# Attention ahead of two mixture layers: a new rank in the list scheduler, another warm-up, later gates, the row factors by one transpose, the last output multiplied out of PSUM

## The chip, the cores and the metric

One core of one Trainium2 chip. The metric is the device time of one execution in microseconds, the median of the runs. All data are fp32; large products are done as three fp32r matmuls on high and low parts.

## The reference

Attention over 4 batches, 8 heads, 576 tokens, head width 64, mixed with a memory read by a gate per head; then two layers on the resulting 2304 x 512 tokens.

```python
scores = scale * q @ k.T;  scores = where(causal, -1e9, scores)
a = exp(scores - scores.max(-1));  a /= a.sum(-1) + 1e-9
local = a @ v
q_p = phi(q)                      # phi(x) = where(x > 0, x, exp(x) - 1) + 1
mem_out = (q_p @ M_prev) / (q_p @ z_prev + 1e-6)
g = 1 / (1 + exp(-beta))
attn = g * mem_out + (1 - g) * local
# layer 1:  h = x @ w_in;  y = (h * tanh(softplus(h))) @ w_out
# layer 2:  tokens with y @ w_skip > 0 go to the best of 8 experts:
#           y + p * (relu(y @ w1[e]) @ w2[e])
```

## The kernel before

**Attention.** The 32 heads are handled as 16 pairs. A pair p has five query tiles t (four of 128 rows for each of the two heads, and one that holds the last 64 rows of both). For each: score (TensorE, S0 does t = 0 and 1), peak (DVE, the negated row maximum, L1053, L1050), expo (ACT, exp with the row sum, L1064). phi1 to phi4 make phi(q) and its product with z. sum0 to sum2 form the row factors rr from the row sums (in two lots: tiles 0 to 2, and 3 and 4): rr[:, 0] is a factor of the whole output row, rr[:, 1] goes into the memory term by place (POOL), which writes phi(q) times factor into the first 64 columns of each row of E. The rows of E are then transposed on TensorE in groups t0, t10, t11, t20, t21, t30, t31, t4, b0 (L1096), each through one of two PSUM buffers pt and evacuated by ACT or DVE into eta and etb (L998, L996). AV0 and AV1 (L1124, 12 and 20 matmuls) multiply with [M; v] and leave the transposed output x^T, 128 x 576, in PSUM px. out_x (xe) copies px to SBUF; scale_x (X, POOL, L1136) multiplies by R; store_x (xo, L1140) stores it to xd in DRAM.

R is rr[:, 0] laid along the free axis and spread over 64 partitions a head. turn_r transposes rr[:, 0] by three matmuls (L1102, L1103), keep_r evacuates the two pieces, store_r writes them to DRAM with two DMAs (L1112, L1113), spread_r reads them back with two broadcasting DMAs (L1117).

Beside that, w_in is converted in 16 tiles (cv: load on SP, scale on POOL, three bit operations on DVE, high part on ACT, low part on POOL, L782 to L827), and the first blocks of x are split.

**What sets the order.** Each step is a task of `Work` with an engine (T TensorE, V DVE, A ACT, G POOL, S SP, VA either of two), an estimated duration, a due time (key), dependencies and, for PSUM, a buffer to take or give ("s" for scores, "t" for pt). While the program is built, `run` repeatedly picks among the first 24 open tasks of each engine the one of smallest rank and appends it to the plan; then all are issued in planned order. The engines execute their own tasks in that order and wait by semaphores. Due times advance by P = 11.2 us a pair, and by 0.8 P a conversion tile.

**Start.** Two 128x512 fp32 matmuls on a zeroed part of E[1] (keep_warm, L1252) run ahead of the first scores. gates0 (ACT) and gates1 (DVE, L977 to L986) form the gates from beta.

**Hand-over.** For the last pair out_x writes into xr, a buffer of the next stage, and POOL multiplies there. Then the attention's SBUF and PSUM are given back: the first GEMM of the mixture (L197 to L199) takes px's PSUM, the units of w_out (uw[4] and on, written by cv.high L824 and cv.low L827) take the attention's SBUF. On ACT, cv.high stands ahead of the first activations of the hidden layer (L209 on); the second GEMM (L249 to L251) begins when the first hidden tile has been split (gh, L232; gl, L235). PSUM holds three tiles ph for the first GEMM.

## Time and profile before

| | us |
|---|---|
| median of 3 runs (lowest, highest) | 914.09 (912.77, 915.0) |
| the profiled execution | 908.42 |
| its span | 906.7 |
| TensorE busy in the span | 841.3 (93%) |
| DVE, ACT, POOL busy | 571.6, 647.9, 287.7 |
| mean granted TensorE clock | 0.987 |

The attention ends near 232 us, the first mixture stage runs to about 690 us, the experts after that. A row of the timeline gives start, duration, engine, line, operation, output <- inputs, and in brackets the idle time of the engine ahead of it and what ended that. "SPq" is SP's DMA queue. A table of windows gives busy time (with the number of instructions) of PE, PEld (weight loads), DVE, ACT and POOL in a stretch. A fp32 matmul shows as two records, a transpose as one.

### The profile page before, as it was taken

What the parts mean: (1) busy time and instruction counts of PE and PEld (TensorE: products, weight loads), DVE (VectorE), ACT (ScalarE), POOL (GpSimd) and SP (SyncE); (2) the same over time, 40 slices, a digit from 0 to 9 for tenths busy, and PEclk for the clock granted to TensorE, in tenths of its full rate; (3) what the DMA queues carried; (4) which work ended last, traced back from release to release, by engine and by line L of the source; (5) the groups of instructions that cost most, each with busy time, mean ns of one, the idle gap of its engine ahead of it and who ended that gap; (6) DMA issues with size and microseconds to landing.
All of it is one profiled execution on the core that took longest, in us unless ns stands there. A gap on an engine that the chain in (4) does not pass through costs nothing. (4 is left out here: it accounts for less than half of the span.)

```text
span 906.7 us, 15121 instructions
## 1 busy us (share of the span) xinstructions
PE 841.3 (93%) x5412; PEld 685.2 (76%) x5412; DVE 571.6 (63%) x1130; ACT 647.9 (71%) x1180; POOL 287.7 (32%) x363
## 2 busy tenths in 40 slices
PE   5889989999799999999999999999878999999995
PEld 3556656666689998999898989888757877777774
DVE  7988888776588833356565747474456765382661
ACT  4777778875688888888989898888865555372551
POOL 6876777754233310110101010111046312121200
PEclk9999999999999999999999999999999999999998
DMA  6666657742333231010111010132227958184610
GB/s 213 198 187 204 202 169 245 216 147 70 124 102 109 97 102 48 24 47 24 48 25 47 25 47 24 48 99 88 82 92 228 357 209 289 41 306 159 196 62 5
DMA packets 53705, 113.45 MB, mean 125 GB/s; under 512 B 12148, under 2 KB 17396, under 8 KB 53600
## 3 DMA queue, kind: packets, MB, share of 16 engines
q1 hardware_dynamic: 43968, 91.22, 31.0%
q0 software_dynamic: 4064, 10.42, 3.5%
q10 hardware_dynamic: 5568, 10.49, 3.2%
q8 instruction: 56, 0.92, 0.4%
q14 instruction: 49, 0.40, 0.1%
HBM read 94.47 MB, written 18.77 MB: 125 GB/s over the span
## 5 line engine op out<-in xcount | busy, mean ns | idle before, releaser
L197 PE MATMUL ph<-xh,u 128*128 128x256 f32 x576 | 164.8, 286 | 0.9 <-DVE xr L996 0.9
L198 PE MATMUL ph<-xl,u 128*128 128x256 f32 x576 | 163.6, 284 | 0.0
L199 PE MATMUL ph<-xh,u 128*128 128x256 f32 x576 | 163.6, 284 | 0.0
L249 PE MATMUL py<-u,gh 128*128 128x512 f32 x288 | 114.9, 399 | 7.4 <-POOL u L827 4.8
L251 PE MATMUL py<-u,gl 128*128 128x512 f32 x288 | 113.9, 395 | 2.2 <-DVE gl L235 2.2
L250 PE MATMUL py<-u,gh 128*128 128x512 f32 x288 | 113.5, 394 | 0.0
L197 PEld LDWEIGHTS ph<-xh,u 128*128 128x128 f32 x576 | 111.0, 193 | 3.2 <-DVE xr L996 1.1
L198 PEld LDWEIGHTS ph<-xl,u 128*128 128x128 f32 x576 | 111.1, 193 | 2.1
L199 PEld LDWEIGHTS ph<-xh,u 128*128 128x128 f32 x576 | 111.0, 193 | 0.0
L235 DVE TENSOR_TENSOR gl<-g,gh 128x512 fp32r<-128x512 f32 x72 | 51.9, 721 | 88.7 <-ACT gh L234 79.2
L225 DVE SCALAR_TENSOR_TENSOR g<-t,g 128x512 f32<-128x512 f32 x72 | 49.8, 692 | 87.1 <-ACT t L221 84.8
L1064 ACT ACTIVATE e<-ps,nm 128x256 f32<-128x256 f32 (+4 forms) x144 | 77.8, 548 | 25.8 <-DVE nm L1053 20.0
L1096 PE MATMUL pt<-ident,e 128*128 128x128 f32 x528 | 76.1, 282 | 7.7 <-ACT eta L998 4.8
L346 POOL DMA_INDIRECT rt<-pay,sl x18 | 19.0, 1055 | 192.6 <-DVE pay L344 189.8
L209 ACT ACTIVATE g<-ph 128x512 f32<-128x512 f32 x72 | 42.8, 595 | 39.8 <-PE ph L199 32.3
L1096 PEld LDWEIGHTS pt<-ident,e 128*128 128x128 f32 x528 | 56.6, 141 | 17.8 <-ACT eta L998 6.7
L249 PEld LDWEIGHTS py<-u,gh 128*128 128x128 f32 x288 | 54.7, 190 | 18.2 <-POOL u L827 5.0
L251 PEld LDWEIGHTS py<-u,gl 128*128 128x128 f32 x288 | 54.3, 189 | 18.6 <-DVE gl L235 7.1
L106 POOL TENSOR_TENSOR xl<-xr,xh 128x256 fp32r<-128x256 f32 x36 | 32.0, 893 | 113.8 <-ACT xh L105 113.6
L827 POOL TENSOR_TENSOR u<-cvf,u 128x512 fp32r<-128x512 f32 x32 | 46.6, 1458 | 57.4 <-ACT u L824 57.4
L250 PEld LDWEIGHTS py<-u,gh 128*128 128x128 f32 x288 | 54.7, 190 | 8.8
L1053 DVE TENSOR_REDUCE nm<-ps 128x2 f32<-128x256 f32 (+1 forms) x64 | 51.3, 817 | 8.2 <-PE ps L1044 6.9
(237 smaller groups left out, 2005.2 us busy)
## 6 DMA issues: line engine op xcount, KB each, us to landing
raw<-w SPq DMA_DIRECT2D x25, 512.0 KB
qk<-qk SPq DMA_DIRECT2D x16, 608.0 KB
raw<-w_in SPq DMA_DIRECT2D x16, 512.0 KB
raw<-w_out SPq DMA_DIRECT2D x16, 512.0 KB
xl<-w SPq DMA_DIRECT2D x16, 512.0 KB
xh<-w SPq DMA_DIRECT2D x15, 512.0 KB
qn<-qn SPq DMA_DIRECT2D x16, 384.0 KB
vx<-vx SPq DMA_DIRECT2D x16, 320.0 KB
```

The lines of the kernel that those rows point to most:

```text
L197: T.matmul(ps[:, f2], win(HI, k, f), hi[:, k], start=(k == 0), stop=False)
L198: T.matmul(ps[:, f2], win(HI, k, f), lo[:, k], start=False, stop=False)
L199: T.matmul(ps[:, f2], win(LO, k, f), hi[:, k], start=False, stop=(k == KD - 1))
L225: V.scalar_tensor_tensor(out=g, in0=t, scalar=ROOT_HALF, in1=g, op0=ALU.add, op1=ALU.mult)
L235: V.tensor_tensor(out=gl, in0=g, in1=gh.bitcast(F32), op=ALU.subtract)
L249: T.matmul(ys[i][t], gh[:, f2, ts], wout(HI, f), start=(f == 0), stop=False)
L250: T.matmul(ys[i][t], gh[:, f2, ts], wout(LO, f), start=False, stop=False)
L251: T.matmul(ys[i][t], gl[:, f2, ts], wout(HI, f), start=False, stop=(f == KF - 1))
L827: self.nc.gpsimd.tensor_tensor(out=lo, in0=self.now.pop(i), in1=hi.bitcast(F32), op=ALU.subtract)
L1053: V.tensor_reduce(out=nm, in_=ps[:, :, o:o + w], axis=AX.X, op=ALU.max, negate=True)
L1064: A.activation(out=E[p % 2][:, k, 64:64 + w], in_=src, func=AF.Exp, bias=nm[:, h:h + 1], scale=1.0, accum_out=SS[p % 2][:, 0, k:k + 1])
L1096: T.transpose(ps[:, c], E[p % 2][:, k, j * 128:(j + 1) * 128], ident)
```

## The change

- The rank of a task was the earliest start in steps of 1/8 us, then the due time; it is now the start plus 0.05 of the due time.
- The warm-up is 12 matmuls identity by identity, issued first; keep_warm and its memset go.
- The load of vx of the first pair becomes the task (0, "lq") with due time -30, and an empty task (0, "ld") tells the planner that q and k of the first pair take 4 us to come. gates0 now stands behind phi1 of the first pair, gates1 behind that pair's maxima of tile 2, with a planned 3.0 us.
- turn_r is one transpose of all nine columns of rr[:, 0], keep_r one evacuation, store_r one DMA; spread_r has four DMAs (a head's four full tiles, and its last 64 rows). Their due times move up from 3.3, 3.7 and 4.0 to 2.0, 2.4 and 2.8 behind the pair's end (t31 has 1.2, t4 2.8, b0 3.2); spread_r's stays at 7.0, with a planned 2.0 us.
- For the last pair out_x is a DVE multiply of px by R, which waits for R too; scale_x falls away there.

```diff
@@ -864,7 +864,7 @@
                     for e in ("V", "A") if eng == "VA" else (eng,):
                         turn = self.SWITCH * (eng == "T" and self.mode(t[2]) != mode)
                         start = max(ready, free[e])
-                        rank = (round((start + turn) * 8), t[0], t[1])
+                        rank = (start + turn + 0.05 * t[0], t[0], t[1])
                         if best is None or rank < best[0]:
                             best = (rank, start, e, eng, t)
             assert best, [ts[0][2] for ts in left.values() if ts]
@@ -909,12 +909,12 @@
         QW = NQT * 128
         KO = QW + 128
         EW = S + 64
-        rd = [dr.tile([2, S], F32, name=f"rd{i}") for i in range(2)]
+        rd = [dr.tile([NS, 128], F32, name=f"rd{i}") for i in range(2)]
         E = [c1.tile([128, NS, EW], F32, name=f"e{i}") for i in range(2)]
         eta = c1.tile([128, 2, 3, 256], F32, name="eta")
         etb = c1.tile([128, 2, 5, 320], F32, name="etb")
         R = [c1.tile([128, S], F32, name=f"r{i}") for i in range(2)]
-        rt_ = c1.tile([NQT, 3, 128], F32, name="rt")
+        rt_ = c1.tile([NS, 128], F32, name="rt")
         MN = [c1.tile([128, NS, D], F32, name=f"mn{i}") for i in range(2)]
         XT = [c1.tile([128, S], F32, name=f"xt{i}") for i in range(2)]
         SS = [c1.tile([128, 2, NS], F32, name=f"ss{i}") for i in range(2)]
@@ -929,6 +929,8 @@
             SP.dma_start(out=t, in_=src[b, m])
             loaded.setdefault(p, {})[nm] = t
 
+        for i in range(12):
+            T.matmul(px[:, 0, 0:128], ident, ident, start=True, stop=True)
         load(0, "qk")
         load(0, "qn")
         bt = c1.tile([128, 12], F32, name="bt")
@@ -1097,24 +1099,20 @@
 
         def turn_r(p):
             pts[p, "r"] = ps = ps_t.tile([128, 4, 128], F32, name="pt")
-            r = rrs.pop(p)[:, 0]
+            T.transpose(ps[0:NS, 0], rrs[p][:, 0], ident)
+
+        def keep_r(e, p):
+            evac(e, rt_, pts.pop((p, "r"))[0:NS, 0])
+
+        def store_r(p):
+            SP.dma_start(out=rd[p % 2], in_=rt_)
+
+        def spread_r(p):
+            d = rd[p % 2]
             for h in range(2):
-                T.transpose(ps[0:NQT, h], r[:, h:2 * NQT:2], ident)
-            T.transpose(ps[0:1, 2], r[:, 2 * NQT:NS], ident)
-
-        def keep_r(e, p):
-            ps = pts.pop((p, "r"))
-            evac(e, rt_[:, 0:2], ps[0:NQT, 0:2])
-            evac(e, rt_[0:1, 2], ps[0:1, 2])
-
-        def store_r(p):
-            d = rd[p % 2]
-            SP.dma_start(out=d[:, 0:QW].rearrange("h (t q) -> t h q", t=NQT), in_=rt_[:, 0:2])
-            SP.dma_start(out=d[:, QW:S].unsqueeze(0), in_=rt_[0:1, 2].rearrange("a (h q) -> a h q", h=2))
-
-        def spread_r(p):
-            for h in range(2):
-                SP.dma_start(out=R[p % 2][HS[h]], in_=rd[p % 2][h:h + 1].to_broadcast([64, S]))
+                SP.dma_start(out=R[p % 2][HS[h], 0:QW].rearrange("p (t q) -> p t q", t=NQT),
+                             in_=d[0:2 * NQT].rearrange("(t h) (a q) -> h a t q", h=2, a=1)[h].to_broadcast([64, NQT, 128]))
+                SP.dma_start(out=R[p % 2][HS[h], QW:S], in_=d[2 * NQT:NS, HS[h]].to_broadcast([64, 64]))
 
         def av(p, i):
             v = loaded[p]["vx"]
@@ -1128,7 +1126,10 @@
                 xt = XT[p % 2]
             else:
                 xt = xs.pool.tile([128, KD, TOK], F32, name="xr", bufs=1).rearrange("p a b -> p (a b)")[:, 0:S]
-            evac(e, xt, pxf[:, 256:256 + S])
+            if p < NPAIR - 1:
+                evac(e, xt, pxf[:, 256:256 + S])
+            else:
+                V.tensor_tensor(out=xt, in0=pxf[:, 256:256 + S], in1=R[p % 2], op=ALU.mult)
             loaded.pop(p)
             xts[p] = xt
 
@@ -1142,9 +1143,10 @@
 
         wk = Work({"s": 2, "t": 2})
         wk.on = {}
-        wk.add(("lv0",), "S", 0.5, 0.5, lambda: load(0, "vx"), lag=3.5)
-        wk.add(("g0",), "A", 0.25, 4.0, gates0)
-        wk.add(("g1",), "V", 2.1, 5.0, gates1, [("g0",)])
+        wk.add((0, "lq"), "S", 0.5, -30.0, lambda: load(0, "vx"), lag=4.5)
+        wk.add((0, "ld"), "G", 0.1, -30.0, lambda: None, lag=4.0)
+        wk.add(("g0",), "A", 0.25, 4.0, gates0, [(0, "f1")])
+        wk.add(("g1",), "V", 3.0, 7.0, gates1, [("g0",), (0, "pk", 2)])
         P = 11.2
         for p in range(NPAIR):
             o = p * P
@@ -1206,18 +1208,20 @@
             tr("b0", P + 3.2, [(p, k, 0) for k in (6, 7, 8)], [key("place1")],
                [(etb[:, :, 0, 128:256], lambda x: x[:, 0:2], 256, prev("AV1")),
                 (etb[:, :, 0, 256:320], lambda x: x[:, 2].rearrange("p (h q) -> p h q", h=2), 128, prev("AV1"))])
-            wk.add(key("r"), "T", 0.35, o + P + 3.3, lambda p=p: turn_r(p), [key("s2", 0), key("s2", 1)], take="t")
-            wk.add(key("re"), "VA", 0.6, o + P + 3.7, lambda e, p=p: keep_r(e, p), [key("r"), prev("rw")], give="t")
-            wk.add(key("rw"), "S", 1.0, o + P + 4.0, lambda p=p: store_r(p), [key("re"), prev2("rs")], lag=3.3)
-            wk.add(key("rs"), "S", 1.0, o + P + 7.0, lambda p=p: spread_r(p), [key("rw"), prev2("X")], lag=3.0)
+            wk.add(key("r"), "T", 0.15, o + P + 2.0, lambda p=p: turn_r(p), [key("s2", 0), key("s2", 1)], take="t")
+            wk.add(key("re"), "VA", 0.25, o + P + 2.4, lambda e, p=p: keep_r(e, p), [key("r"), prev("rw")], give="t")
+            wk.add(key("rw"), "S", 0.5, o + P + 2.8, lambda p=p: store_r(p), [key("re"), prev2("rs")], lag=3.3)
+            wk.add(key("rs"), "S", 2.0, o + P + 7.0, lambda p=p: spread_r(p), [key("rw"), prev2("X")], lag=3.0)
             ev = lambda *ns: [key(n, "e", 0) for n in ns]
             wk.add(key("AV0"), "T", 1.05, o + 10.5, lambda p=p: av(p, 0), ev("t0", "t10", "t11") + [prev("xe"), key("lv")])
             wk.add(key("AV1"), "T", 2.5, o + P + 5.1, lambda p=p: av(p, 1),
                    ev("t20", "t21", "t30", "t31", "t4", "b0") + [key("t4", "e", 1), key("b0", "e", 1)] + [prev("xe"), key("lv")])
-            wk.add(key("xe"), "VA", {"V": 0.7, "A": 0.6}, o + P + 8.0, lambda e, p=p: out_x(e, p),
-                   [key("AV0"), key("AV1")] + [("xs", 1, KD - 1)] * (p == NPAIR - 1) + [prev2("xo")])
-            wk.add(key("X"), "G", 1.7, o + P + 11.0, lambda p=p: scale_x(p), [key("xe"), key("rs")])
-            wk.add(key("xo"), "S", 0.5, o + P + 13.0, lambda p=p: store_x(p), [key("X")], lag=2.5)
+            end = p == NPAIR - 1
+            wk.add(key("xe"), "V" if end else "VA", {"V": 0.7, "A": 0.6}, o + P + 8.0, lambda e, p=p: out_x(e, p),
+                   [key("AV0"), key("AV1")] + [("xs", 1, KD - 1), key("rs")] * end + [prev2("xo")])
+            if not end:
+                wk.add(key("X"), "G", 1.5, o + P + 11.0, lambda p=p: scale_x(p), [key("xe"), key("rs")])
+            wk.add(key("xo"), "S", 0.5, o + P + 13.0, lambda p=p: store_x(p), [key("X"), key("xe")], lag=2.5)
 
         NCV = 16
         CVP = 0.8 * P
@@ -1246,14 +1250,6 @@
             for k in range(KD):
                 wk.add(("xs", x, k), "G", 1.2, t + 7.0 + 1.5 * k, lambda x=x, k=k: xs.split(x, k), [("xl", x)] + [("xs", x, k - 1)] * (k > 0))
 
-        wtile = E[1].rearrange("p a b -> p (a b)")
-
-        def keep_warm():
-            T.matmul(px[:, 0], wtile[:, 0:128], wtile[:, 0:512], start=True, stop=True)
-
-        V.memset(wtile[:, 0:512], 0.0)
-        for _ in range(2):
-            keep_warm()
         wk.run()
         return wk
```

## Rows read from the trace of the kernel before

**Rows 1.** Table of windows: us, busy us of each engine (instructions), granted clock, DMA share, GB/s

```profile
45.00:90.00 45.00, 40.63 (x343) 27.38 (x344) 39.04 (x69) 34.38 (x102) 31.07 (x48) 1.00 0.62 198
...
190.00:200.00 10.00, 10.00 (x89) 6.81 (x88) 7.02 (x15) 7.04 (x22) 5.89 (x12) 1.00 0.46 145
...
260.00:280.00 20.00, 20.00 (x131) 18.33 (x131) 14.88 (x25) 16.14 (x23) 5.08 (x7) 1.00 0.31 88
```

**Rows 2.** Timeline, TensorE: AV1 of the first, ninth and fifteenth of sixteen pairs

```profile
32.77 2.49 PE L1124 MATMUL px<-etb,vx 128*64 128x320 f32 x20 [0.52 <-DVE etb L996]
...
147.39 2.49 PE L1124 MATMUL px<-etb,vx 128*64 128x320 f32 x20
...
220.33 2.49 PE L1124 MATMUL px<-etb,vx 128*64 128x320 f32 x20
```

**Rows 3.** Timeline, the hand-over from attention to the mixture, 227 to 250 us

```profile
227.36 1.01 PE L1096 MATMUL pt<-ident,e 128*128 128x128 f32 x7 [0.35 <-DVE etb L996]
...
228.96 0.38 PE L1102 MATMUL pt<-ident,rr 128*4 128x128 f32 x2 [0.59 <-DVE etb L996]
...
229.38 2.48 PE L1124 MATMUL px<-etb,vx 128*64 128x320 f32 x20
...
231.89 1.11 SPq L1117 DMA_DIRECT2D r<-rd  x2
...
231.91 0.76 DVE L996 COPY xr<-px 128x576 f32<-128x576 f32 x1 [1.82 <-PE px L1124]
...
232.72 0.39 PE L197 MATMUL ph<-xh,u 128*128 128x256 f32 x1 [0.86 <-DVE xr L996]
...
235.44 1.44 POOL L1136 TENSOR_TENSOR xr<-xr,r 128x576 f32<-128x576 f32 x1 [8.06 <-DMA r<-rd]
...
236.91 0.63 ACT L824 ACTIVATE u<-cvf 128x512 fp32r<-128x512 f32 x1 [6.76 <-POOL xr L1136]
...
247.73 1.49 DVE L232 CAST gh<-g 128x512 fp32r<-128x512 f32 x1
...
249.32 0.77 PE L249 MATMUL py<-u,gh 128*128 128x512 f32 x1 [4.82 <-POOL u L827]
```

**Rows 4.** Table of windows of one microsecond behind TensorE's idle time

```profile
251.00:252.00 1.00, 1.00 (x3) 0.73 (x3) 0.96 (x2) 0.98 (x2) 0.09 (x1) 0.50 0.00 0
```

**Rows 5.** Timeline, the start of the kernel, 0 to 16 us

```profile
1.10 0.29 POOL masks.py:199 TENSOR_SCALAR_AFFINE_SELECT ident<-ident 128x128 f32<-128x128 f32 x1
...
4.93 0.88 POOL L1004 TENSOR_SCALAR qk<-qk,nums,one 128x640 f32<-128x640 f32 x1 [0.98 <-DMA qk<-qk]
...
5.78 3.78 PE L1252 MATMUL px<-e 128*128 128x512 f32 x4 [5.78 <-DVE e L1254]
...
7.83 0.17 DVE L977 TENSOR_SCALAR gates<-gates 128x12 f32<-128x12 f32 x1
...
9.49 0.66 PE L1041 MATMUL ps<-qk 64*128 64x128 f32 x4
...
11.54 1.01 DVE L1053 TENSOR_REDUCE nm<-ps 128x2 f32<-128x256 f32 x2
...
12.66 0.37 ACT L1064 ACTIVATE e<-ps,nm 128x128 f32<-128x128 f32 x1 [5.43 <-DVE nm L1053]
...
15.71 1.22 DVE L1053 TENSOR_REDUCE nm<-ps 128x2 f32<-128x1024 f32 x1 [1.29 <-PE ps L1044]
```

**Rows 6.** Groups by line, shapes apart, 22 to 218 us: the factors' two evacuations on ACT

```profile
L998 ACT ACTIVATE rt<-pt 4x256 f32<-4x256 f32 x11 | 4.0, 365 | 2.9 <-PE pt L1103 2.9
...
L998 ACT ACTIVATE rt<-pt 1x128 f32<-1x128 f32 x11 | 2.7, 249 | 0.0
```

**Rows 7.** One line's instructions, L1117: ns min/median/max, first and last start

```profile
L1117 SPq DMA_DIRECT2D r<-rd x32: 460/581/776, 36.6 to 232.4; - x32
```

**Rows 8.** Who waited for whom, 22 to 218 us: us in total, times, longest

```profile
PE pt L1102 <- DVE etb L996: 3.7, 4, 1.2
...
ACT mn L1007 <- DMA qn<-qn: 1.6, 2, 0.9
```

## The prediction

> **What bounds the kernel now.** I read the table of windows first. In the attention TensorE shows 9.0 of every 10 us busy in 45:90 and 10 in 190:200; VectorE shows 8.7 of 10 while the conversion of w_in runs beside it and 7.0 after; in the first mixture stage (260:280) TensorE has no gap at all [rows 1]. So a microsecond saved before 250 us reaches the end if it lets TensorE start that long run earlier; from there the work follows TensorE and keeps what was saved. The second view is the timeline of the twenty-matmul AV1 group, one per pair: the sixteen starts run from 32.77 us (first) over 147.39 (ninth) and 220.33 (fifteenth) to 229.38 (last) [rows 2, 3]. The first eight steps take 114.6 us, 14.3 each; the next six 72.9, 12.2 each. The conversion's work sits in the first eight. Third, the hand-over to the mixture [rows 3] and the clock behind it [rows 4]; fourth, the start [rows 5]; fifth, the costs of the factor path, turn_r to spread_r, and of the loads that share its queue [rows 6 to 8].
>
> **Handing over: the last x^T.** Before, DVE copies px to xr at 231.91 and the R DMA, issued at 231.89, lands only at 235.44, where POOL multiplies (1.44 us); ACT's first conversion L824 writes memory that the attention frees, so it waits for that and starts at 236.91 [rows 3]. TensorE starts its first GEMM at 232.72, does four of them, and then idles 4.82 us until 249.32 for the first hidden tile: the matmul at 249.32 follows the end of the DVE cast gh (247.73 + 1.49 = 249.22) [rows 3], which hangs on ACT, busy without a gap from 236.91. From ACT's start to that matmul are 12.4 us. [...]
> After, one DVE multiply does the copy and the product; px is released, and ACT let go, by its end. Its price: the 128x576 copy here took 0.76 [rows 3]; I take 0.8. But it now waits for R too. Where is R then? turn_r has due time 2.0, behind t31 (1.2) and ahead of t4 (2.8) and b0 (3.2); it uses one of the same two PSUM buffers, and where several can start the lower due time wins. So for the last pair it stands where t4 and b0 start now, at 227.36, not 228.96 [rows 3]. The steps after it, by their rows: 2.7 from the transpose to the first spread (228.96 to 231.89 is 2.9 now, less one evacuation of 0.25), four spreads instead of two at 0.58 each (2.3), and 2.4 from the end of the issue to the data (231.89 + 1.11 to 235.44) [rows 3, 6, 7]. That is 227.36 + 2.7 + 2.3 + 2.4 = 234.8. AV1 ends at 231.9, perhaps 0.4 later because t4 now finds its buffer one turn later. So R ends last, by about 2.5 us; the multiply ends at 235.5 and ACT starts there instead of at 236.91: 1.4 us won. TensorE's first GEMM starts 2.8 later than now, at 235.5; four of them take 11.6, to 247.1, and the hidden tile is there at 235.5 + 12.4 = 247.9. [...] **-2.5.**
> [...]
>
> **Start.** Now the two warm-up matmuls wait for a memset of E[1], hold TensorE from 5.78 to 9.56, and the first scores, whose q is scaled at 5.81, start at 9.49 [rows 5]. A matmul of this type shows as two records; the four took 3.78 us, 0.94 for 512 columns or 0.24 for 128 [rows 5], where a 128-column record of the same type, a transpose, takes 0.14 late in the attention (seven in 1.01) [rows 3]. After, 12 matmuls on the identity are 24 records of 128 columns: 0.14 to 0.24 each, 3.4 to 5.7 in all, from 1.4 (the identity is made by 1.39), so to 4.8 or 7.1. The first scores come at 5.9 to 7.2: 2.3 to 3.6 earlier. DVE next: the gates sit from 7.83 to 11.54 ahead of the first maximum [rows 5]; they go behind the maxima of tiles 0 to 2. Then the first maximum is at about 8.0 (behind phi2, which ends at 7.9), the first exp at 8.5 instead of 12.66, and the scores of tile 3, which wait for those exps, some 4 us earlier too. But the 3.7 us of gates are moved, not removed: they are now ahead of tile 3's maximum or sum2, and DVE's last idle time ahead of tile 3's maximum, at 15.71, is 1.29 [rows 5]; from phi2 on it has no other. So the gain is 1.3 if DVE's total decides, 4.2 if the chain of exps does. I take 2.3, nearer to DVE's, as it is the busier engine in this stretch. The removed memset lay in idle time: nothing. vx of pair 0 goes out ahead of qk of pair 1; that is needed 4 us later than it comes: nothing; if not, 1 us. **-2.3.**
>
> **Factors in one transpose.** Now three transposes per pair, and the next group starts 0.42 behind the first (228.96 to 229.38); one will take 0.14 [rows 3]. 0.28 by 16 = 4.5 us of TensorE. Two evacuations, 0.37 and 0.25 on ACT, become one of 128 columns like the second: 0.37 by 16 = 5.9 us over ACT and DVE [rows 6]. Beside that, turn_r waited 3.7 us in all behind DVE for its buffer [rows 8]. Against it: standing ahead of t4 it takes t4's buffer for a turn, at most about 0.4 us a pair, 6.4 in all. Ends -8.2 and +6.4; TensorE is the nearest thing to a bound, but it has other work between most of these, so I take less than half of its own saving: **-2.0.** On SP one small store goes and two spreads of 0.58 come: at most 1.2 us more a pair [rows 7], and what is queued behind (the loads of the next pairs, x stores, raw weights) is later by that. Moved up, the spread also makes them wait with SP for the factors' store to land, as it did before at its old place. The loads are early now (ACT's waits for qn are 1.6 us in 196) [rows 8], so nothing; without this cover 16 by 0.6 to 1.2, 10 to 19 us.
>
> **The rank.** Before: earliest start in steps of 1/8 us, then due time. After: start + 0.05 x due time. An operation due 20 us earlier may keep an engine waiting 1 us for it. The pairs fall behind their due times (11.2 us a pair planned, 12.2 to 14.3 taken [rows 2]), the conversion (8.96 us a tile) does not, so the new rank puts attention ahead of conversion on DVE. This may even out the pace of the first half, or leave engines idle for work that isn't there yet. The trace can't show the new order. One end: the first eight steps at 12.8 instead of 14.3, -12 (12.2 would be -17, but the conversion has to go somewhere). Other end: one more wait a pair of the size of those at turn_r (3.7 us in four, 0.9 each [rows 8]), fourteen times, +13. I take **0**.
>
> **Sum.** -2.5 - 2.3 - 2.0 = -6.8. The profiled execution took 908.42 (span 906.7, 1.7 around it) and gives 901.6, 0.75% less. The median of the runs is 914.09, 0.6% above the profiled one; the same 0.75% off gives **907.2**.
>
> **Rivals.**
> A. The forecast, 901 to 911.
> B. The rank evens out the first half: the conversion moves into the later pairs, where DVE is at 7 of 10 [rows 1]. For: 14.3 against 12.2 us a pair. Against: TensorE is at 9 of 10 already in both halves. 8 of the 12 us more: 899 (range 894 to 901).
> [...]
> D. Slower, by one mechanism: the in-order engines are made to wait for older work under the new rank, in the steady state of the attention, 0.9 us more a pair as priced above, 13 us in all: 914.1 - 6.8 + 13 = 920. It decides from 0.5 us a pair (6.8 / 14); beyond 0.7 it shows as slower. For: the plan's own pace is shorter than the real one, so the planned starts by which it ranks are off. Against: only operations many microseconds older gain that right.
> E. The change doesn't do what it says: turn_r still lands behind b0, since its inputs (sum2 of tiles 3 and 4) come late. Then the hand-over is 1.6 us worse, about 909; inside A's range.
>
> **Chances.** A (with E) 0.48, B 0.13, C 0.22, D 0.17. What the measurement can tell from no change is about 0.3%, 2.7 us. Faster: A and B, 0.61; within: C, 0.22; slower: D, 0.17. The range leaves out most of D and the far half of B: 897 to 917.
>
> **What would show it.** In the changed profile: first scores at 6 to 7 us, first exp near 8.5; the AV1 starts as a ladder, with the first 2 us earlier and steps no longer than now (D: steps longer; B: the first eight near 12.5); the L1102 group once a pair ahead of t4; at the end DVE's multiply waiting on DMA r<-rd by about 2.5 us, the ACT L824 start within 0.1 us of its end, TensorE's idle ahead of its first second-GEMM matmul below 1.5 us, and the clock at 1.00 there. Wrong would be: waits ahead of the maxima or transposes grown by 0.5 us a pair, DVE's total idle grown in 45:135, or R landing after 236 us relative to AV1's end at 232.

## The result, and the profile after

The changed kernel takes **918.84 us** (median of 22 runs, 913.93 to 923.98); the kernel before, run beside it, 914.74 (22 runs). The ratio is 1.0056, 95% interval 1.004 to 1.0071: **slower by 0.56%**, where the prediction said 907.2 and its range ended at 917. The profiled execution took 918.89 (span 917.2), against 908.42 before.

Read the profile from the end of the attention backwards and forwards. The attention did become shorter. AV1 of the first, ninth and fifteenth pair of the changed kernel on TensorE's timeline, to be laid beside [rows 2]:

```profile
29.84 2.48 PE L1122 MATMUL px<-etb,vx 128*64 128x320 f32 x20
...
135.96 2.49 PE L1122 MATMUL px<-etb,vx 128*64 128x320 f32 x20
...
213.18 2.48 PE L1122 MATMUL px<-etb,vx 128*64 128x320 f32 x20
```

The first AV1 comes 2.9 us earlier, the ninth 11.4, the fifteenth 7.2. The first eight steps now take 13.3 us each (14.3 before), the next six 12.9 (12.2 before): the pace was evened out. The table of windows from the first to the ninth AV1 says the same (columns as in [rows 1]: length, then busy time of TensorE, its weight loads, VectorE, ScalarE, GpSimd). The kernel before:

```profile
33.00:147.00 114.00, 102.25 (x872) 68.61 (x869) 101.25 (x164) 85.99 (x251) 86.37 (x126) 1.00 0.63 201
```

and the changed one:

```profile
30.00:136.00 106.00, 100.83 (x830) 66.37 (x828) 98.57 (x157) 80.16 (x229) 82.76 (x118) 1.00 0.68 205
```

TensorE was idle for 11.8 us in the first and is for 5.2 in the second.

The hand-over, timeline of the changed kernel, the answer to [rows 3]:

```profile
221.27 0.27 PE L1102 MATMUL pt<-ident,rr 128*9 128x128 f32 x1 [0.44 <-DVE etb L998]
...
223.35 2.49 PE L1122 MATMUL px<-etb,vx 128*64 128x320 f32 x20 [0.78 <-DVE etb L998]
...
225.07 0.61 SPq L1115 DMA_DIRECT2D r<-rd  x1
...
227.78 0.76 DVE L1132 TENSOR_TENSOR xr<-px,r 128x576 f32<-128x576 f32 x1 [4.49 <-DMA r<-rd]
...
228.59 0.38 PE L197 MATMUL ph<-xh,u 128*128 128x256 f32 x1 [2.76 <-DVE xr L1132]
...
228.69 0.64 ACT L824 ACTIVATE u<-cvf 128x512 fp32r<-128x512 f32 x1 [4.28 <-DVE xr L1132]
...
231.76 0.60 ACT L209 ACTIVATE g<-ph 128x512 f32<-128x512 f32 x1 [1.86 <-PE ph L199]
...
243.81 0.63 PE L249 MATMUL py<-u,gh 128*128 128x512 f32 x1 [3.45 <-POOL u L827]
```

Line 249 starts 5.5 us earlier than before (243.81 against 249.32). So the sum of -6.8 was not far off where I had drawn its end, the start of the mixture. I laid the mixture's and the experts' matmuls of both kernels side by side (3616 records in each): the lead of 5.3 us holds up to 445 us and has shrunk to 1.2 at 735. One microsecond of it goes where TensorE waits for ScalarE, which it does not do there in the kernel before, and 1.7 where the clock is granted at 0.50 for 3.4 us; the two rows of the changed kernel, one of the timeline and one of the table of windows (the column behind POOL's is the granted clock):

```profile
445.73 0.50 PE L249 MATMUL py<-u,gh 128*128 128x512 f32 x1 [1.06 <-ACT gh L234]
...
588.70:592.10 3.40, 3.40 (x10) 2.70 (x9) 2.83 (x7) 3.31 (x6) 0.00 (x0) 0.50 0.00 0
```

Then two places in the experts take 5.3 + 7.0 us (matmuls 2880 to 2940 and 3120 to 3240 take 20.4 and 33.0 us, in the kernel before 15.1 and 26.0), and at the end the changed kernel is 10.5 late. The two places on TensorE's timeline of the changed kernel (the bracket: idle time ahead of the instruction, and what ended it; PEq is TensorE's sequencer, "issue" that it waited for nothing the profile shows):

```profile
752.37 0.79 PE L490 MATMUL ph<-u,ah 128*128 128x512 f32 x1 [7.30 <-issue]
...
808.17 0.47 PE L490 MATMUL ph<-u,ah 128*128 128x512 f32 x1 [2.35 <-PEq L756]
...
813.66 0.79 PE L491 MATMUL ph<-u,ah 128*128 128x512 f32 x1 [4.33 <-issue]
```

and in its table of windows:

```profile
740.00:760.00 20.00, 12.70 (x55) 10.02 (x54) 10.61 (x12) 8.83 (x12) 2.93 (x3) 0.83 0.76 266
800.00:820.00 20.00, 13.32 (x57) 10.35 (x56) 10.76 (x12) 9.16 (x13) 2.92 (x3) 0.83 0.76 257
```

The same two views of the kernel before:

```profile
749.10 0.47 PE L490 MATMUL ph<-u,ah 128*128 128x512 f32 x1 [2.80 <-PEq L756]
...
804.18 0.48 PE L490 MATMUL ph<-u,ah 128*128 128x512 f32 x1 [1.60 <-PEq L756]
```

```profile
740.00:760.00 20.00, 17.20 (x78) 13.58 (x77) 14.88 (x16) 13.39 (x18) 3.45 (x3) 0.91 0.86 295
800.00:820.00 20.00, 18.40 (x89) 14.68 (x88) 17.00 (x19) 13.31 (x17) 4.68 (x4) 1.00 0.84 280
```

All engines do less work in these windows of the changed kernel, TensorE 4.5 and 5.1 us less, and its clock is granted at 0.83. Nothing that the change edits runs there. Both places lie behind line 756, where the nested `If`s of an expert are closed: each time a branch is taken and jumps over blocks that this expert does not need.

The DMA table of a window shows what differs (queue and kind, packets, MB, share of the engines). Queue 8 carries instructions, 16384 bytes at a time (58 packets, 0.95 MB on the changed kernel's page). In the 13 us from 744 on, the changed kernel:

```profile
q8 instruction: 3, 0.05, 1.5%
```

and in the 13 us from 745 on, the kernel before:

```profile
q8 instruction: 2, 0.03, 1.2%
```

By the single packets, the changed kernel loads at 744.48, 750.19 and 755.18; its branch ends at 746.99, TensorE has nothing to execute until the second load is in (751.15) and goes on at 752.37. The kernel before loads at 746.34 and 750.89 and goes on at once behind the branch.

**Theory.** The change takes 37 instructions out of TensorE's program ahead of the mixture (the traces show 3418 executed there and 3455 before, behind it 7548 in both), and I take a code load to hold 256 of them, an estimate from the traces: in the changed kernel the 22 loads from 234 to 674 us come one per 255.7 executed instructions on average, in the kernel before those from 235 to 667 us one per 255.8. So all branch targets in the experts lie 37 places further up in their blocks. In the changed kernel these two taken branches land a few instructions ahead of a block's end: the load that such a branch waits for brings next to nothing, and the following load is waited for in full. **Rivals:** the stalls come from the weights' transfers, which meet the experts at another time; or from the attention's changes themselves.

### The profile page after: what moved, and what is told of

It is laid out like the page before. It is cut to its first block, busy times and chain, and to the rows that moved or that the text cites. A ratio compares the mean times of both kernels' runs of the same rounds, so it can differ in the third digit from the quotient of the medians.

```text
span 917.2 us, 15085 instructions
## 1 busy us (share of the span) xinstructions
PE 849.9 (93%) x5400; PEld 690.2 (75%) x5400; DVE 570.0 (62%) x1125; ACT 645.1 (70%) x1168; POOL 283.4 (31%) x362
## 4 chain that ended last, share of the span: by engine, by line
PE 36%; ACT 21%; issue 18%; DMA 11%; DVE 8%; POOL 4%; ACTq 1%; SPq 1%; POOLq 0%; another core or an unknown queue 0%; DVEq 0%
DMA out<-cvf,ids 4%; PE pt L1098 4%; PE ph L197 4%; PE ph L199 4%; PE ph L198 4%; DMA cvt<-yd,ids 4%; PE py L249 4%; PE py L251 4%; PE py L250 3%; PE px L1122 3%; PE ps L1043 3%; ACT L217 3%; ACT t L220 2%; ACT L222 2%; ACT t L210 2%
## 5 line engine op out<-in xcount | busy, mean ns | idle before, releaser
L197 PE MATMUL ph<-xh,u 128*128 128x256 f32 x576 | 164.8, 286 | 2.8 <-DVE xr L1132 2.8
L249 PE MATMUL py<-u,gh 128*128 128x512 f32 x288 | 115.7, 402 | 7.0 <-POOL u L827 3.5
L197 PEld LDWEIGHTS ph<-xh,u 128*128 128x128 f32 x576 | 111.0, 193 | 5.1 <-DVE xr L1132 3.0
L1066 ACT ACTIVATE e<-ps,nm 128x128 f32<-128x128 f32 (+2 forms) x144 | 78.0, 552 | 20.8 <-DVE nm L1055 10.3
L209 ACT ACTIVATE g<-ph 128x512 f32<-128x512 f32 x72 | 42.8, 595 | 46.3 <-PE ph L199 36.6
L249 PEld LDWEIGHTS py<-u,gh 128*128 128x128 f32 x288 | 55.2, 192 | 17.8 <-ACT gh L234 4.9
L494 ACT ACTIVATE h<-ph 128x512 f32<-128x512 f32 x32 | 19.1, 596 | 64.0 <-PE ph L492 56.0
```

The costliest lines, as they stand in the source:

```text
L197: T.matmul(ps[:, f2], win(HI, k, f), hi[:, k], start=(k == 0), stop=False)
L209: A.activation(out=g, in_=hs[s], func=AF.Silu)
L249: T.matmul(ys[i][t], gh[:, f2, ts], wout(HI, f), start=(f == 0), stop=False)
L1066: A.activation(out=E[p % 2][:, k, 64:64 + w], in_=src, func=AF.Exp, bias=nm[:, h:h + 1], scale=1.0, accum_out=SS[p % 2][:, 0, k:k + 1])
```

## Experiments

To shift code without touching anything else, some variants have one-column matmuls into an unread PSUM buffer behind the attention, nine of them in the first:

```
         wk.run()
+        ps = ps_t.tile([128, 4, 128], F32, name="pt")
+        for i in range(9):
+            T.matmul(ps[0:1, 0, 0:1], ident[:, 0:1], ident[:, 0:1], start=True, stop=True)
```

Places are counted in the compiled programs, modulo 256, from the first instruction, without the marks of jump targets (no trace shows one executed). "First" and "second" are the two branches at which the changed kernel stood still; others are taken ahead of them and between them. The first lands at 229 in the kernel before and at 192 in the changed one, the second at 221 and 184. The expectations below were written with a count in which the places fall too little from one expert to the next; there the second is six higher (227 and 190, in other runs 191, 195 and 203).

| run | what | median us | ratio to before, 95% | first / second target |
|---|---|---|---|---|
| before_again | the kernel before, once more | 914.32 | 1.0012 (0.9982 to 1.0041) | 229 / 221 |
| after_pad36 | change, nine matmuls behind the attention | 903.95 | 0.990 (0.9855 to 0.9945) | 229 / 221 |
| before_pad220 | before, 55 matmuls at the start | 921.37 | 1.0097 (1.0066 to 1.0129) | 193 / 185 |
| after_pad4 | change, one matmul | 914.88 | 1.0027 (0.9998 to 1.0056) | 197 / 189 |
| after_pad12 | change, three matmuls | 912.67 | 1.0006 (0.9981 to 1.0031) | 205 / 197 |
| after_pad256 | change, 64 matmuls | 912.99 (one run) | | 193 / 185 |
| rank_only | before with the new rank | 911.47 | 1.0001 (0.9971 to 1.003) | 205 / 197 |
| rank_pad24 | rank_only, six matmuls | **901.56** | 0.9885 (0.9849 to 0.9921) | 230 / 222 |
| no_end_pad36 | change, old hand-over, nine matmuls | 902.23 | 0.9884 (0.9822 to 0.9947) | 229 / 221 |
| r_early_pad36 | change, last factors sooner, nine matmuls | 902.07 | 0.9887 (0.9817 to 0.9957) | 229 / 221 |
| no_start | change, old start | 903.75 (one run) | | 154 / 146 |
| no_factor | change, old factors | 904.49 (one run) | | 247 / 239 |
| no_end | change, old hand-over | 914.57 (one run) | | 192 / 184 |

no_start, no_factor and no_end were executed once each; what their parts are worth is read by stage.

**Is it the place of the code?**

> The kernel before, unchanged, for a second profile. In the profiles so far the changed kernel reaches the first matmul of the second GEMM at 243.8 us, 5.5 sooner than before, and then loses all of it and more, most in the expert stage, where TensorE stands still for 7.3 and 4.3 us behind two skipped blocks without waiting for any semaphore. If the profile of before (908.4, under its median of 914.7) was typical in its expert stage, this profile again has no idle time over 3 us of TensorE there. If stalls there come at random, it may have one.

> The changed kernel with nine one-column matmuls (36 instructions of TensorE) behind the attention, where TensorE waits for R anyway. Theory 1, the place of the code: the targets of the taken branches lie in the changed kernel 37 instructions earlier than before, 188 to 200 modulo 256, just ahead of the end of a 16-KB block of instructions, so that a taken branch has to wait for two block loads in a row; with the pad they lie at 225 to 237 as before. Then the first matmul of the second GEMM stays at about 243.8 to 244.3, the two idle times (7.3 and 4.3 us) shrink to those of before (2.8 and 1.6), and the median comes down by 8 to 11 us, to 908 to 911, some 0.4 to 0.7% faster than before. Rival, the time: the stalls come from when the weights' transfers run; then moving the code changes nothing, and it stays near 918.

> The kernel before with 55 one-column matmuls (220 instructions) at its very start, which puts the branch targets at 189 to 201 modulo 256, as in the changed kernel. They may delay the first scores by up to 3 us. Theory 1: TensorE gets idle times of over 4 us without a semaphore behind the skipped blocks of the experts, and the time goes up by 8 to 14 us over before, to 923 to 931. Rival (the time of the transfers): only the delay at the start, 914 to 918, and no such idle times.

The kernel before stayed where it was, without an idle time over 3 us in the experts. Nine matmuls made the changed kernel 15 us *faster* (1.6% by the two ratios), more than the 8 to 11 that I had expected; its gaps at the two branches are 2.06 and 2.61 us. The kernel before with its targets moved to where the changed kernel has them (one place off) became 0.97% slower, 8.5 us over the kernel beside it, at the low end of the 8 to 14 that I had expected and with 921.37 under the 923 to 931: its first branch does not stall, and no idle time there reaches 4 us. Part of the 0.97% is its later start (first GEMM at 237.44 against 232.72); the rest goes with a stall at the second branch, on its timeline:

```profile
816.92 0.58 PE L490 MATMUL ph<-u,ah 128*128 128x512 f32 x1 [3.74 <-issue]
```

So it is not the change's plan: work added in one kernel takes the stall away, and work added in the other brings it. The added work also moves the times by some microseconds, so the rival of the weights' timing needs the next runs.

**Is it the place, or merely more instructions?**

> The changed kernel with 64 one-column matmuls (256 instructions of TensorE, as many as one code load brings) behind the attention, where the faster variant had nine (36). The experts' branches then land at the same place of a 256-instruction block as without any (181 to 201 in place of 180 to 200). Theory 1 (where the branch lands decides): the stalls of the changed kernel stay, 4 to 9 us at the first taken branch and 3 to 5 us at the second, and the kernel takes 914 to 922. Theory 2 (any extra instructions or a delay in front of the mixture loosen the stall): gaps of at most 3 us, and 904 to 908.

With a whole block more, which leaves the targets where they were but for one place, the second stall stayed (3.16 us) and the time is 912.99, not 904 to 908 (the place alone would have given 914 to 922); but the first was gone (1.90, with two loads). I had expected both. One place further, 193 for 192, decides at the first branch, as it does in before_pad220, which has no stall there either. (Three more kernels bear the place out: no_end, with the changed kernel's 192 and 184, stalls for 8.69 and 3.23 us; no_start at 154 and 146 and no_factor at 247 and 239 have no gap over 2.93 in the experts.) That suggested an edge, and the next run took it up:

> The changed kernel with one single one-column matmul behind the attention: with its wait it moves the experts' code by 5 instructions. Where the first and second skipped blocks are jumped over, the branch lands at place 192 and 190 of a 256-instruction block in the changed kernel (both stall, 7.3 and 4.3 us, with three code loads in a row), at 193 and 191 with 256 matmul instructions more (the first has two loads and no stall, the second three loads and 3.2 us), at 205 and 203 with the rank alone (two loads each). Theory 1 (a code block ends between 192 and 193; a branch that lands in the last few instructions of a block pays two loads one behind the other): here they land at 197 and 195, so each shows two loads and a gap of at most 3 us, and the kernel takes 903 to 907. Theory 2 (no sharp edge; the nearer to 200 the worse, or the loads come as chance has it): stalls of 3 to 8 us stay, and 910 to 918.

Timeline of after_pad4 at the two branches:

```profile
747.44 0.47 PE L490 MATMUL ph<-u,ah 128*128 128x512 f32 x1 [2.52 <-PEq L756]
...
805.90 0.59 PE L491 MATMUL ph<-u,ah 128*128 128x512 f32 x1 [3.62 <-issue]
```

and its code loads in the 13 us from 744 and from 798 on:

```profile
q8 instruction: 2, 0.03, 1.0%
...
q8 instruction: 3, 0.05, 1.7%
```

Half a hit. The first stall went, with its third load, and with it 4.0 us of the median; the second did not, so the time, 914.88, is that of theory 2. The reason is the count: the second branch lands here at 189, not at 195. With the places of the table one edge, between 192 and 193, fits both branches in all kernels, and it tells how many matmuls TensorE can still do before it needs the next block. A landing begins with a wait for a semaphore, and a matmul takes two instructions, a weight load and the matmul: from 192 on none fits, from 184 four, from 185 three, from 189 one. The traces have just that. The stall stands ahead of the first matmul behind the landing at 192 (changed kernel, no_end), ahead of the fifth at 184 (both again), ahead of the fourth at 185 (before_pad220, after_pad256) and ahead of the second at 189 (here: line 491 at 805.90; the order is 490, 491, 492, 490, 491). Where the branch itself took only 0.34 us and no code was loaded ahead of its end, as at 788.54 in the changed kernel (the next load starts at 789.53), a landing at 184 has no such stall (0.44 us ahead of line 490 at 792.61, nothing behind it).

The last run tried it with places at which a kernel had already been seen:

> The changed kernel with three one-column matmuls behind the attention, 13 instructions with their wait: the branches land at 205 and 203, at the same places as with the new rank alone. Theory 1 (the place decides, branch by branch): two code loads and a gap of at most 3.5 us at the first and second taken branch, where the changed kernel has 7.3 and 4.3; but two stalls of 1.5 to 2.5 us near 870 and 888, as with the rank alone (867 and 885); in all 907 to 912, between the 903.95 with 36 instructions more and the 914.88 with 5 more. Theory 2 (the late stalls belong to the rank's plan or to chance): none over 1.3 us behind 860, and 903 to 906. Theory 3 (5 and 13 instructions alike, since the stall needs 36): a stall of 3 us or more at the second branch, and 913 to 917.

Timeline of after_pad12 at the four branches:

```profile
746.47 0.47 PE L490 MATMUL ph<-u,ah 128*128 128x512 f32 x1 [2.17 <-PEq L756]
...
800.39 0.47 PE L490 MATMUL ph<-u,ah 128*128 128x512 f32 x1 [2.13 <-PEq L756]
...
868.88 0.39 PE L491 MATMUL ph<-u,ah 128*128 128x512 f32 x1 [2.17 <-issue]
...
885.42 0.59 PE L490 MATMUL ph<-u,ah 128*128 128x512 f32 x1 [2.56 <-issue]
```

and its code loads in the 13 us from 797 on:

```profile
q8 instruction: 2, 0.03, 1.1%
```

Timeline of rank_only, whose targets are at the same places, at the two late ones:

```profile
867.07 0.39 PE L491 MATMUL ph<-u,ah 128*128 128x512 f32 x1 [2.12 <-issue]
...
884.71 0.56 PE L490 MATMUL ph<-u,ah 128*128 128x512 f32 x1 [2.07 <-issue]
```

The first two stalls are gone and two late ones have come, in another kernel, at the places of rank_only. Those late branches land at 187 (from where a further jump leads to 190) and 185 in both kernels, and both stall ahead of the second matmul (line 491) and ahead of the fourth (line 490), as the edge has it. The time, 912.67, is 0.7 above the range of theory 1. From the 3481st of the 3616 matmuls to the last it takes 36.9 us, rank_only 36.8, all others 29.2 to 32.0. The place decides, branch by branch, whatever the kernel and the time: that leaves the weights' timing only the length of a stall.

**What is each part worth?** Read by the end of the last AV1 and the start of line 249, ahead of the experts.

> The kernel before with the new rank alone. It tells the rank's part of the 5.5 us that the whole change gains up to the first matmul of the second GEMM (249.3 before). If the rank evens out the pace, that matmul comes at 245 or sooner; if the rank holds engines idle, later than 251; if it is neutral, at 249 +- 1. Its branch targets lie at 193 to 213 modulo 256 (24 instructions fewer): by theory 1 the first experts are past the block's end and the last ones may stall as in the changed kernel.

> The kernel before with the new rank alone and six one-column matmuls behind the attention (24 instructions), which put the experts' branches at 218 to 238 of a block, as in the kernel before; without them they stood at 193 to 213 and the kernel took 911.47. Theory 1 (the rank carries the whole gain of the attention, and the late stalls at 867 and 885 came from where the branches land): 903.5 to 907, line 249 starts 242 to 243.5, no gap over 3 us in the experts. Theory 2 (rank without start, factors and hand-over loses something in the experts for another reason): 909 to 912.

> The changed kernel with the start of the kernel before: the warm-up of two wide matmuls, the head's vx load as a planned step of its own, and the two gate chains in their old places; rank, factors and hand-over stay changed. Read by the start of the last multiplication of the attention (the last AV1) and by the first matmul of line 249, since the experts' stage differs by where its code lies. In the changed kernel AV1 of the first pair starts at 29.84, the last one ends at 225.84, and line 249 starts at 243.81; with the new rank alone the last ends at 225.08 and line 249 starts at 242.61. Theory 1 (the new start is worth nothing behind the rank, because the first maxima meet the same queue of VectorE): last AV1 ends within 1 us of 225.8. Theory 2 (the start is worth its forecast 2.3 us): it ends at 227.5 to 229. Theory 3 (the start costs, since TensorE is idle for 6.5 us behind the longer warm-up and has half its clock up to 18.7): it ends at 223 to 225.

> The changed kernel with the old factors: three transposes, two copies out of PSUM, two stores and two spreading transfers a pair, at their old due times; the start and the hand-over stay changed. Read by the end of the last AV1 and by the first matmul of line 249. In the changed kernel the steps from AV1 of the first pair to that of the ninth are 13.3 us each, and the next six 12.9. Theory 1 (the factors' cost lies beside other work): last AV1 ends within 1 us of 225.8, and line 249 comes up to 1 us later, since the factors of the last pair come later. Theory 2 (worth the forecast 2.0 us along the pairs): the last AV1 ends at 227.3 to 228.5. Theory 3 (the new factors cost, by four spreading transfers in SP's queue where two stood, 0.6 us each): it ends at 223.5 to 224.8.

> The changed kernel with the old hand-over of the last pair: the last x^T is copied out of PSUM and multiplied by the factors on GpSimd; the rest stays changed. Read from the end of the last AV1 (225.84 in the changed kernel) to the first matmul of line 249 (243.81): 17.97 there, 17.46 in the kernel before, 17.53 with the new rank alone. Theory 1 (the multiplication out of PSUM saves nothing here, because it waits 2.0 us for the factors that the old path needs 1.0 us later, and because ScalarE's chain now hangs on the first GEMM, which starts only with it): 17.5 to 18.5. Theory 2 (the new path saves the 2.5 us of the forecast and something else in the changed kernel costs it): 19.5 to 21. Theory 3 (the new path costs): 16 to 17.2.

> The changed kernel with the old hand-over (copy out of PSUM, multiplied on GpSimd) and nine one-column matmuls behind the attention, so that the branches land where the kernel before has them. Theory 1 (the old hand-over beats the new one by the 1.9 us that TensorE waited for the factors, and by 1.5 more where its clock falls in that wait): line 249 starts 16.0 to 16.6 us after the last AV1 ends, and 901 to 903 against 903.95 with the new one in the same place. Theory 2 (what the hand-over wins is given back in the mixture, whose steps wait for the blocks' weights): 903.5 to 905.

> The changed kernel with the factors of the last pair due 3 us or more sooner on TensorE, VectorE, SP (ahead of the last pair's other steps), and with nine one-column matmuls behind the attention, which move the experts' code by 36 instructions to where the kernel before has it. Theory 1 (the hand-over waited for the factors: multiplication at 227.78, 1.94 after the last AV1 ended at 225.84): the multiplication now starts within 0.4 us of the last AV1's end, line 249 starts 16.0 to 16.6 us after that end where the changed kernel took 17.97, and the kernel takes 901 to 903.5 (903.95 with the same 36 instructions and the factors as they were). Theory 2 (something else holds line 249, such as the blocks' weights or ScalarE's chain): 17.5 to 18 as before and 903 to 905. Theory 3 (the sooner factors push other steps of the last pair back by as much): the last AV1 ends 1 us or more later and the time is 904 to 906.

```
-  rank = (round((start + turn) * 8), t[0], t[1])
+  rank = (start + turn + 0.05 * t[0], t[0], t[1])          # rank_only, on the kernel before

-  T.matmul(px[:, 0, 0:128], ident, ident, ...)  x12        # no_start: the old two wide ones,
-  lq at -30; gates1 behind ("pk", 2)                       #   lv0 at 0.5, gates1 behind gates0
-  T.transpose(ps[0:NS, 0], rrs[p][:, 0], ident)            # no_factor: the old turn_r, keep_r,
                                                            #   store_r, spread_r and due times
-  V.tensor_tensor(out=xt, in0=pxf[...], in1=R[p % 2], ...) # no_end: evac, then POOL's multiply

-  wk.add(key("r"), "T", 0.15, o + P + 2.0, ...             # r_early, for the last pair:
+  wk.add(key("r"), "T", 0.15, o + 8.6, ...                 #   re, rw, rs likewise sooner
```

| kernel | last AV1 ends | first L197 | first L209 | L249 |
|---|---|---|---|---|
| before | 231.86 | 232.72 | 238.00 | 249.32 |
| changed | 225.84 | 228.59 | 231.76 | 243.81 |
| rank_only | 225.09 | 225.95 | 231.30 | 242.61 |
| rank_pad24 | 223.35 | 224.29 | 229.59 | 240.88 |
| no_start | 225.14 | 227.84 | 232.50 | 244.55 |
| no_factor | 223.92 | 228.33 | 233.00 | 245.05 |
| no_end | 224.07 | 224.93 | 228.49 | 240.16 |
| r_early_pad36 | 224.97 | 225.91 | 229.06 | 241.11 |

The **rank** alone moves the end of the last AV1 by 6.8 us, more than the whole change does (6.0); in rank_pad24, the same plan, it is 8.5. The timeline of rank_only, first, ninth and fifteenth AV1:

```profile
29.71 2.49 PE L1124 MATMUL px<-etb,vx 128*64 128x320 f32 x20 [0.71 <-DVE etb L996]
...
134.40 2.49 PE L1124 MATMUL px<-etb,vx 128*64 128x320 f32 x20
...
212.43 2.49 PE L1124 MATMUL px<-etb,vx 128*64 128x320 f32 x20
```

13.1 us a step in the first half, 13.0 in the next six. Its table of windows for the first half:

```profile
30.00:134.00 104.00, 101.30 (x842) 67.60 (x839) 99.34 (x157) 80.05 (x230) 80.35 (x119) 1.00 0.64 202
```

Of TensorE's 11.8 us of idle time in that half 2.7 are left, and it is 9.9 us shorter; 3.1 more were won ahead of the first AV1, and the steps behind the ninth gave 6.2 back. With its code out of the way of the edges it is as fast as anything here: 901.56, a little below the range that I gave (903.5 to 907), and line 249 at 240.88 comes sooner than the 242 to 243.5. The same plan with the edges took 911.47.

The **start** and the **factors** are worth nothing that these runs can tell. The executions of the changed kernel, its four padded forms and no_end, which run the same program up to there, end the last AV1 between 224.07 and 226.88; without the start it is 225.14 (theory 1), without the factors 223.92 (theory 3 by its number, but only 0.15 below that scatter, so I can't tell it from theory 1). Why the start fails, the timeline of the changed kernel shows, the answer to [rows 5]:

```profile
1.45 4.64 PE L933 MATMUL px<-ident 128*128 128x128 f32 x24 [1.45 <-POOL ident masks.py:199]
...
6.02 0.49 PE L1043 MATMUL ps<-qk 64*128 64x128 f32 x4
...
7.83 1.88 DVE L1055 TENSOR_REDUCE nm<-ps 128x2 f32<-128x256 f32 x3
...
11.48 0.68 ACT L1009 ACTIVATE mn<-qn 128x576 f32<-128x576 f32 x1 [4.25 <-DMA qn<-qn]
...
12.79 0.35 ACT L1066 ACTIVATE e<-ps,nm 128x128 f32<-128x128 f32 x1
...
14.54 2.08 PE L1043 MATMUL ps<-qk 64*128 64x512 f32 x4 [6.51 <-ACT e L1066]
```

The scores and the first maximum came as forecast (6.02 and 7.83). But the first exp is at 12.79, where it was at 12.66: ScalarE had phi of the *next* pair queued ahead of it and stood 4.25 us waiting for that pair's qn to land. TensorE, the scores of tiles 0 to 2 done, idled 6.51 us.

The **hand-over**: no_end has line 249 at 240.16, 16.1 us behind the last AV1's end, where the changed kernel takes 18.0. The old copy-then-multiply, *with the change's sooner factors*, beats multiplying out of PSUM by 1.9: theory 3. Its rows on the timeline:

```profile
224.93 0.39 PE L197 MATMUL ph<-xh,u 128*128 128x256 f32 x1 [0.86 <-DVE xr L998]
...
227.38 0.63 ACT L824 ACTIVATE u<-cvf 128x512 fp32r<-128x512 f32 x1 [4.72 <-POOL xr L1134]
...
240.16 0.77 PE L249 MATMUL py<-u,gh 128*128 128x512 f32 x1 [3.46 <-POOL u L827]
```

TensorE starts 1.9 us sooner behind AV1 (0.86 for 2.75), because the copy waits for no factor; ScalarE starts later but not late enough to matter. With the factors sooner still (r_early_pad36) the multiplication starts 0.04 behind the last AV1 and line 249 comes 16.15 behind it, inside the 16.0 to 16.6 expected (no_end_pad36 takes 16.15 too). So what costs is the wait for the factors and not the multiplication out of PSUM:

```profile
225.01 0.76 DVE L1132 TENSOR_TENSOR xr<-px,r 128x576 f32<-128x576 f32 x1 [2.77 <-PE px L1122]
...
241.11 0.47 PE L249 MATMUL py<-u,gh 128*128 128x512 f32 x1 [3.45 <-POOL u L827]
```

In the whole time that advantage cannot be told from after_pad36 (0.9887 against 0.990, intervals overlapping), and none of the three fastest kernels from another.

## Why the prediction was wrong, point by point

**What bounds the kernel: the step that failed.** "From there the work follows TensorE and keeps what was saved" carried the whole forecast from 250 us to the end. It did not hold. In the mixture 4.1 of the 5.3 us were lost, at a wait for ScalarE and at falls of the clock; why they came is open. In the experts TensorE's own instruction stream had a cost by place, which my sum put at nothing: TensorE stood still for 7.30 us at the first branch and 2.35 + 4.33 at the second, where the kernel before has 2.80 and 1.60, and with the clock of 0.50 behind it (749.20 to 755.90 and 810.60 to 817.30) the two stretches took 12.3 us more. With the place put back the changed kernel takes 903.95, inside the range (897 to 917) and 3.3 below the 907.2. No rival of mine had this, and a view of the kernel before could have: its longest idle times in the experts already read "<-PEq L756", the branch, and the profile's third part lists the instruction queue. Rival D had the sign but not the mechanism: the attention became shorter, not 13 us longer.

The traces show what a load costs where. In code without branches nothing that shows: ten loads of 16384 bytes start between 256 and 436 us of the changed kernel, and TensorE is busy for 179.09 of these 180 us. At line 756 the branches in whose time a load starts take 3.36 to 5.56 us in the changed kernel and 3.32 to 6.02 in the kernel before, the others 0.07 to 0.34. The second load, right behind such a branch, is what the place decides: the first branch of the changed kernel ends at 746.99, and TensorE goes on 5.38 us later, behind the load of 750.19.

**Hand-over (-2.5 forecast).** By its steps: turn_r ahead of t4 and b0, as said (2.1 us ahead of AV1's start; 0.4 before [rows 3]), so rival E is out. R was ready 1.9 us behind AV1's end; I had 2.5 to 2.9, and the four spreads cost 0.6 each, as costed. ScalarE started 2.85 behind AV1's end where it was 5.05: 2.2 won, 1.4 forecast. The step that failed is that the hidden tile is there 12.4 behind ScalarE's start ("at 235.5 + 12.4 = 247.9"): it came 15.1 behind. The 12.4 was a distance in which ScalarE had its first L209 input waiting; now L209 waits 1.86 us for the first GEMM, which starts 1.9 us later because it, too, waits for R. In all eight rows of the table line 249 comes 11.3 to 12.1 behind the first L209, and L209 itself is the later of ScalarE's first L824 + 1.1 and TensorE's first L197 + 3.2 (4.7 where the clock is granted at 0.50). AV1 to line 249 thus took 17.97, against 17.46 before: +0.5 instead of -2.5. What the -2.5 holds beyond ScalarE's 1.4 was put down to the clock, a term that no run shows: ahead of line 249 TensorE idles 3.45 us in the changed kernel and 3.45 to 4.91 in the seven others read there (4.82 before [rows 3]), and behind it the changed kernel's clock is granted at 0.50 from 244.00 to 247.30, as the kernel before's is from 248.90 to 252.20 (table of windows):

```profile
244.00:247.00 3.00, 3.00 (x8) 2.19 (x8) 2.93 (x4) 2.97 (x5) 1.57 (x1) 0.50 0.13 53
```

In no_start it even fell earlier as well, inside the first GEMMs behind the idle time (window 229:232 of no_start):

```profile
229.00:232.00 3.00, 3.00 (x16) 3.00 (x16) 2.93 (x4) 0.15 (x1) 0.99 (x1) 0.50 0.78 253
```

and of the changed kernel:

```profile
229.00:232.00 3.00, 3.00 (x27) 3.00 (x27) 2.93 (x4) 1.14 (x3) 1.35 (x1) 1.00 0.57 198
```

16 matmuls against 27 at the same code. Of the executions that idle there, with the new hand-over, it fell so in five (no_start, no_factor, after_pad4, after_pad12, after_pad36) and not in two (the changed kernel, after_pad256). It costs 1.5 us: line 249 comes 16.7 behind the first L197 in those, 15.2 in these. From the end of the last spread's issue (225.68) to the multiplication are 2.1 us, before 2.4 [rows 3]. The smaller packets of the new spread (512 and 256 bytes, 2304 before) cost nothing there that shows.

**Start (-2.3).** The warm-up's 4.64 us and the scores at 6.02 were right. The choice between "DVE's total" and "the chain of exps" missed the queue that decided: ScalarE's, in order, behind a wait for a transfer. It is worth nothing that shows; the first AV1's 2.9 us earlier are the rank's (29.71 in rank_only).

**Factors in one transpose (-2.0).** The record of the one transpose is 0.27 long, not 0.14; its evacuation took 0.26, as said. The saving lay beside other work: the end of AV1 is 223.92 without it, below the others. Its being sooner helps only at the hand-over: line 249 comes 21.1 behind the last AV1's end without it (no_factor, 1.5 of that the clock's), 18.0 with it in the changed kernel and 16.1 with it and the old path (no_end).

**The rank (0, rival B -8).** Rival B was right in mechanism and nearly in size: -6.8 at the end of the attention, the first half's steps at 13.1 us instead of 14.3, and the conversion paid for in the later ones, 13.0 for 12.2; 3.1 of the 6.8 lie ahead of the first AV1, which B did not have. I had given it 0.13, against it that TensorE was at 9 of 10 busy in both halves. But the tenth that was left is 11.8 us over the first half, more than the whole forecast; the order of priorities was what it waited for.

So the forecast up to line 249 came out near (-5.5 for -6.8) by luck, from terms that were wrong one by one: rank -6.8 for 0, start and factors about 0 for -4.3 (+0.8 in these two executions, inside their scatter), hand-over +0.5 for -2.5. That after_pad36 lies inside the range is the same luck.

**The place of the loss, in sum.** From after_pad36 to the changed kernel the medians differ by 14.9 us. In the profiled executions (spans 917.2 and 907.9; that of after_pad36 was its slowest run) the stretches with the two branches, matmuls 2880 to 2940 and 3120 to 3240 of the 3616, take 20.4 + 33.0 us and 14.5 + 28.3: 10.6 us, the clock of 0.50 behind the stall included. What the medians hold beyond that I can't assign: between 580 and 700 us the clock fell to 0.50 four times in some executions (from 588.7, 636.5, 663.8 and 677.5 us in the changed kernel, 3.4 us each) and once in others, behind the same idle times, and matmuls 2160 to 2760 take 130.0 us in the changed kernel and in after_pad36 and 124.0 in r_early_pad36. Why is open.

## To carry over

In a program with branches that are taken at run time, adding or removing instructions anywhere ahead of them moves their targets, and here that cost or gave 1 to 1.6% that had nothing to do with the edit: compare the idle times behind the branches first, and before judging an edit put the targets back where they were, with a few instructions that do nothing. A list scheduler's order of priorities can be worth more than all the hand-made edits around it, as it was here (rank_pad24, the rank alone, is as fast as anything); cost it by the pace of its slowest stretch. And a distance read off a trace (the 12.4 above) is only a bound for the chain that was late there: move that chain, and ask which one is next.

## What the hardware showed that I had not expected

- One no-op matmul more (5 instructions) behind the attention took away a stall of 7.3 us more than 500 us later; 13 took away a second and brought two others; 36 left none over 3.0 us (r_early_pad36).
- At the stalls two code loads in a row are 5.7 us apart in the experts' first half, where weights stream (744.48 and 750.19, 805.65 and 811.38 in the changed kernel; queue 1 takes 67.4% and 64.8% of the DMA engines in the 13 us around them), and 3.1 near the end, where they have stopped (861.41 and 864.49 in rank_only; no packet of queue 1 from 860 to 872). The stall behind the landing is about that distance less the work that the rest of the target's block holds: 5.38 us in the changed kernel at 192, with no matmul left in the block, and 4.33 at 184, with four (1.16 us).
- The clock fell or stayed behind nearly equal idle times: after 2.76 us in the changed kernel's hand-over it stayed at 1.00, after 2.71 in no_start it went to 0.50 (both from 229 to 232 us).
